# Squared sums for the weights' scales, a two-step split of v, and a list-scheduled first block in an attention and mixture-of-experts kernel

## The chip, the cores and the metric

The kernel runs on one core of a Trainium2 chip. The core has five engines with an instruction queue each: TensorE (PE in the profile, with its weight loads apart as PEld), VectorE (DVE), ScalarE (ACT), GpSimd (POOL) and SyncE (SP), which issues the DMAs here. An engine takes its instructions strictly in the order in which they were written into its queue, and waits where an operand isn't there yet. The metric is the device time of one execution in microseconds (us); the time of a kernel is the median of its runs.

## What is computed

Attention on 4 batches, 8 heads, 768 positions and 64 elements a head: each position sees its neighbours (closer than 16) and a summary of each block of 32 keys. Its output, 3072 rows of 512, goes through four dense experts that are mixed by given weights.

```python
scores_l = scale * q @ k.T                      # only where |i - j| < 16
scores_s = scale * q @ k_sum.T + log(32)        # k_sum: the maximum over each block of 32
a = softmax([scores_l, scores_s])
x = a @ [v, v_sum]                              # v_sum: the mean over each block
p = domain_probs / domain_probs.sum(-1)
for e in range(4):
    out += p[:, e:e + 1] * (relu(x @ w1[e]) @ w2[e])
```

The result has to be close to float32, so the kernel splits operands into a high and a low part of a shorter type, and makes three matrix products in place of one.

## The kernel before

Attention works in pieces: a batch, a block of 96 queries, and a group of four of the eight heads; there are 64, numbered `n` in the order of time, and names such as `ms`, `psc`, `px` carry that number. The experts work on blocks of 384 rows. Blocks 0 and 1 (batch 0) are plain, with operands in 32-bit types: experts 0 and 1 on block 0, then 1 and 0 on block 1. The other work is done for a pair of blocks at once, four experts each, with seven products in place of eight (`SEVEN`) and operands in 16 bits. These need a scale for each matrix, so that the high and low parts fit, and the products are scaled back at the end.

**The first block.** The first eight pieces (`first_tokens`, function `piece`) stand before all expert work and have a form of their own, in plain float32. For a piece TensorE makes scores into two PSUM tiles `psc`, one for the heads in partitions 0 to 63 ("half" 0) and one for those in 64 to 127 (half 1); each score tile gets two matmuls a head, against the keys (128 columns) and against the summary (24 columns). VectorE takes the maximum (`ms`, `nb`), ScalarE the exponential, TensorE turns it (`pT`), multiplies it with v (`pav`), VectorE divides (`xt`), TensorE turns that back, and ScalarE and VectorE split it into `xh` and `xl`. What comes when in this part was written out by hand as keys (`KEYS`, `STEPS`, `T0`), by which the steps are sorted.

**The weights' scales.** `scan` loads a quarter megabyte of a weight matrix into a tile `ws` and takes its largest magnitude into a column of `wmax` (`largest`). After the sixteen tiles of an expert, `scales_of_weights` reduces `wmax` to `wm`, and `scales` makes a maximum over all partitions of it: TensorE transposes `wm` into a PSUM tile `pmw`, VectorE reduces and spreads it, TensorE sends it to all partitions, and eight small VectorE operations make a power of two and its inverse. The experts come in the order 2, 3, 1, 0. With that scale `w1` (tiles `wx`, into `w1g`) and `w2` (tiles `wr`, into `w2g` or `w2s`) are scaled and split.

**v.** For batches 1 to 3 (48 pieces) `stage_a` scales v in place on ScalarE, casts it on ScalarE and makes the low part on GpSimd.

**Order.** Every call is recorded as a `Step` in `program`, and `order_of` makes the queues from that. Each step has a due time that is worked out backwards from TensorE's order, and costs by a table (`takes`, `lasts`); a forward pass picks on each engine the ready step that is due first, a backward pass gives new due times, and of so many rounds the order that ends first by its own reckoning is kept. `in_order` says up to which step an engine keeps the order of the program. In the kernel before that was the whole first block on PE, ACT, DVE and POOL, and the loads of `first_tokens` on SP. Buffers of one tag (`wr` has four, `x` 14, `av` two PSUM banks, `sc` two) are handed out in the order of the program. `ENDS` says how far attention has got at the end of each phase of expert work, `XFREE` up to which piece the odd pieces take tiles from the tag `x`, and `early` how long before a pair's work `x_operands` begins to prepare its operands.

Of the kernel before, what the change touches and what calls it, by code (L numbers as in the profile page):

```python
# [36 lines left out]
SHIFT = 1.12  # L37
ENDS = (17.52,26.5,36.5,53.0,72.0,74.0)
WARM = 11

KEYS = (1.38, 3.85, 1.13, 11.28, 5.91, 6.72, 13.44, 18.09, 21.41, 52.74, 24.82, 23.32, 21.81, 24.25, 59.33, 71.64, 6.83, 9.12)
T0 = 2.57
STEPS = (-1.19, -0.88, 0.85, 0.66, 1.27, 1.34, 1.82, 1.84, 3.16, 3.29, 3.37, 3.66, 3.72, 5.09, 5.84, 6.11, 6.57, 6.89)
CHUNKS = 2
XFREE = 28
NX = 14
# [18 lines left out]
WAIT = dict(PE=53, ACT=33, DVE=33, POOL=76, SP=28)  # L65
SPARE, SPARE_DMA, LANES = 0.1, 300.0, 8
ROUNDS = 10


def columns(ap):  # L70
    return math.prod(n for _, n in ap.ap[1:])
# [15 lines left out]
class Step:  # L87


    def __init__(self, key, issue, op, a, kw):  # L90
        self.key, self.issue = key, issue
        written = [kw[k] for k in ("out", "accum_out") if k in kw]
        read = [x for k, x in kw.items() if k not in ("out", "accum_out")]
        if "out" in kw:
            read += a
        else:
            written.insert(0, a[0])
            read += a[1:]
# [3 lines left out]
        self.behind, self.ahead, self.tiles, self.glued = {}, [], [], False  # L102

    def moved(self):
# [5 lines left out]
    def PE(self, op, kw):  # L110
        n, w = self.moved(), self.read[0]
        if op == "transpose":
            return 95.0, 260.0
        if w.dtype == F32:
            return 65.0 + 1.75 * n, 230.0 + 1.75 * n
        if columns(w) == D:
            return 22.0 + 0.18 * n, 215.0 + 0.25 * n
        t = max(70.0, 0.453 * n) + 15.0 * (n < 200) if w.dtype == F32R else max(45.0, 0.4235 * n)
        t *= 0.65 if w.ap[0][1] == D else 1.0
        return t, t + 165.0  # L120

    def ACT(self, op, kw):
        n = self.moved()
        if op == "activation" and "accum_out" in kw:
            return 420.0 * (1 + SPARE), 560.0 + 420.0 * SPARE
        if op == "mul" and len(self.read) > 1:
# [37 lines left out]
def order_of(steps, bufs, early):  # L164
# [133 lines left out]
    def forward(rank):  # L298
        run = Run(rank, queue, [sum(head[m] != head[n] for m in steps[n].behind) for n in every])
        run.after_slot = lambda n: WAIT[keys[n]]  # L300
        lanes, wire, order = [0.0] * LANES, 0.0, []
        start, end = [0.0] * len(steps), [0.0] * len(steps)
        run.begin()
        while len(order) < len(steps):
            t, k, group = run.next(lambda k: max(run.free[k], lanes[0] + WAIT[k]) if k == "SP" else run.free[k])
            for n in group:
                s = steps[n]
                order.append(n)
                start[n] = t
                if k == "SP":  # L310
# [50 lines left out]
def attn_moe(ctx: ExitStack, tc: tile.TileContext, qvL, qv0, v0L, kD, kT, vT, w1L, w2L, dpL, cst, out):  # L361
# [55 lines left out]

    X_TOP, W1_TOP = 4.0, 0.25
    V_TOP = 256.0
# [5 lines left out]
    def largest(e, fc, which, raw):  # L425
        V.tensor_reduce(
            wmax[:, e, which, fc : fc + 1], raw, axis=AX.X, op=ALU.max, apply_absolute_value=True
        )

# [25 lines left out]
    def scales_of_weights(e):  # L455
        m = sb.tile([P, 2], F32, name=f"wm{e}", tag="wm")
        V.tensor_reduce(m, wmax[:, e], axis=AX.X, op=ALU.max)
        s, back = scales(f"w{e}", m, 2)
        one = const.tile([P, 2], F32, name=f"one{e}")
        V.tensor_scalar_mul(one[:, 0:1], s[:, 0:1], W1_TOP)  # L460
        V.scalar_tensor_tensor(
            one[:, 1:2], back[:, 0:1], 1.0 / (X_TOP * W1_TOP), back[:, 1:2], op0=ALU.mult, op1=ALU.mult
        )
        scale_w[e], back_w[e] = (one[:, 0:1], s[:, 1:2]), one[:, 1:2]

# [142 lines left out]
    def stage_a(n):  # L608
# [205 lines left out]
    def first_tokens(units):  # L814
# [104 lines left out]
        def piece(n, m, s):  # L919
# [11 lines left out]

            def scores(half):
                t["psc", half] = ps_sc.tile([P, 2, 256], F32, name=f"psc{n}_{half}", tag="sc")
                for j in (half, half + 2):
                    o = t["psc", half][:QB, j // 2, :]
                    r = slice((j % 2) * D, (j % 2 + 1) * D)
                    PE.matmul(
                        o[:, 0:KW], qr[r, j // 2, :], kch[2 * g + j // 2][r, w0 : w0 + KW], start=True, stop=True
                    )
                    PE.matmul(o[:, KW:KA], qr[r, j // 2, :], ksr[r, 2 * g + j // 2, :], start=True, stop=True)  # L940

# [62 lines left out]
            def x_part(w):  # L1004
# [6 lines left out]
            steps = (  # L1011
                (v_ones,), (scores, 0), (scores, 1), (maxima, 0), (maxima, 1), (exps, 0), (exps, 1),
                (summary,), (turn, 0), (turn, 1), (turn_summary,), (turned,), (turned_summary,),
# [612 lines left out]
    for (tbs, experts), end in zip(plan, ENDS):  # L1626
# [9 lines left out]
        for e in experts[:1] if paired else experts:  # L1636
# [4 lines left out]
            for us, pace in units:  # L1641
# [84 lines left out]
```

## Time and profile before

| | |
|---|---|
| runs | 1080.18, 1080.83, 1082.72 us; median 1080.83 us |
| profiled execution | 1079.39 us, its span 1077.5 us |
| TensorE clock | 0.995 of full speed in the mean |
| DMA | 194.95 MB, mean 181 GB/s |

The page of the profile gives for each engine its busy time; a view by windows gives the same for chosen stretches, with the granted TensorE clock; the view of waits lists who waited for whom; the view of groups gives the mean duration of one kind of instruction; and the timeline gives instructions with start and duration in us, and in brackets the idle time of the engine ahead of them and what ended it. Almost every instruction has the line L373, the line of a helper, so groups are told apart by the names of tiles.

### The profile page before, as it was taken

To read this page: it belongs to the slowest core of one execution; us is meant where nothing else is said; L and a number is where in the kernel's file an instruction comes from. 1 tells how busy PE (TensorE), PEld (TensorE's weight loads), DVE (VectorE), ACT (ScalarE), POOL (GpSimd) and SP (SyncE) were. 2 spreads that over 40 slices of the span, in tenths; PEclk is the share of its full clock that TensorE was granted. 3 is DMA by queue.
4 is the path that set the end of the run, shared out by engine and by line. 5 is a ranking of instruction groups with operands and counts; after the bars stand their busy time and mean duration, and the time that the engine had idled before them with its cause. 6 is when DMAs were issued, how large, how long until landed. Compare 5 with 4: busy or idle time off the path is not lost.

```text
span 1077.5 us, 22082 instructions
## 1 busy us (share of the span) xinstructions
PE 1051.8 (98%) x7497; PEld 707.7 (66%) x7497; DVE 866.0 (80%) x2102; ACT 730.2 (68%) x1992; POOL 607.2 (56%) x716
## 2 busy tenths in 40 slices
PE   9988999899999999999999999999999999999998
PEld 7977888654554555555555568686775567686867
DVE  6898889988877867988988897998767775969473
ACT  5776688887864744976977796988545763748170
POOL 2599588877743211852856887896532352717050
PEclk9999999989999999999999999999999999999999
DMA  8789887987888889789676664657422440424001
GB/s 287 212 202 244 227 220 198 274 270 198 240 245 253 253 232 254 220 268 263 207 231 170 167 176 126 176 163 217 116 83 89 135 149 16 162 66 151 1 15 59
DMA packets 172897, 194.95 MB, mean 181 GB/s; under 512 B 80368, under 2 KB 117232, under 8 KB 172784
## 3 DMA queue, kind: packets, MB, share of 16 engines
q1 hardware_dynamic: 172784, 193.55, 62.3%
q8 instruction: 58, 0.95, 0.4%
q14 instruction: 55, 0.45, 0.1%
HBM read 141.33 MB, written 35.65 MB: 164 GB/s over the span
## 4 chain that ended last, share of the span: by engine, by line
PE 66%; DVE 5%; POOL 2%; ACT 2%; DMA 1%; issue 1%; SPq 0%; DVEq 0%; POOLq 0%; ACTq 0%
PE po L373 16%; PE phb L373 13%; PE pha L373 8%; PE pob L373 7%; PE poa L373 5%; PE phd L373 4%; PE phc L373 4%; PE poc L373 3%; PE pod L373 2%; PE psc L373 2%; PE px L373 1%; POOL w2g L373 1%; DVE wr L373 1%; DMA wr<-in_w2L 1%; ACT ms L373 0%
## 5 line engine op out<-in xcount | busy, mean ns | idle before, releaser
L373 PEld LDWEIGHTS <-w1g 128*128 128x128 f16 x2352 | 229.2, 98 | 174.2 <-issue 13.0
L373 PEld LDWEIGHTS <-h 128*128 128x128 f16 x1764 | 171.0, 98 | 115.9 <-issue 0.5
L373 PE MATMUL po<-w2s,h 128*128 128x512 f16 x1008 | 239.6, 379 | 0.0
L373 PE MATMUL phb<-x_t,w1g 128*128 128x384 f16 x1008 | 195.3, 327 | 4.6 <-DVE phc L373 1.9
L373 POOL TENSOR_TENSOR w2g<-wr,w2g 128x512 f16<-128x512 f32 (+1 forms) x80 | 90.1, 1133 | 114.3 <-ACT w2g L373 112.1
L373 PE MATMUL pha<-x,w1g 128*128 128x384 f16 x672 | 133.3, 329 | 2.9 <-DVE nb L373 2.9
L373 ACT ACTIVATE ms<-ms,nb 96x152 f32<-96x152 f32 x256 | 104.0, 414 | 15.5 <-DVE nb L373 15.2
L373 PEld LDWEIGHTS <-hs 128*128 128x128 f16 x1008 | 98.0, 98 | 12.7 <-issue 0.4
L373 POOL TENSOR_TENSOR v<-qv,v 128x256 f16<-128x256 f32 (+1 forms) x56 | 45.7, 816 | 104.6 <-ACT v L373 89.7
L373 DVE CUSTOM_DVE_ANT_0 ms<-psc,c_sb 96x152 f32<-96x152 f32 x256 | 69.1, 305 | 31.3 <-PE psc L373 30.5
L373 POOL TENSOR_TENSOR h<-r,h 128x384 f16<-128x384 f32 x56 | 57.1, 1025 | 54.1 <-ACT h L373 51.5
L373 ACT CAST w2g<-wr 128x512 f16<-128x512 f32 (+1 forms) x112 | 61.6, 562 | 32.2 <-DVE wr L373 18.7
L373 POOL TENSOR_TENSOR w<-wr,w 128x512 fp32r<-128x512 f32 x48 | 65.3, 1368 | 26.2 <-ACT w L373 20.3
L373 DVE TENSOR_TENSOR aw<-ms,aw 96x512 f16<-96x512 f32 (+1 forms) x104 | 69.7, 686 | 6.3 <-ACT aw L373 6.3
L373 PE MATMUL ph<-xh,w 128*128 128x384 f32 x256 | 69.4, 343 | 5.1 <-ACT w L373 3.6
L373 PE MATMUL phd<-x_t,w1g 128*128 128x384 f16 x336 | 65.6, 326 | 2.6 <-POOL w1g L373 1.7
L373 PE MATMUL phc<-x,w1g 128*128 128x384 f16 x336 | 66.1, 326 | 0.0
L373 PE MATMUL poa<-w2g,h 128*128 128x256 f16 x504 | 65.4, 273 | 0.4 <-DVE nb L373 0.4
L373 PE MATMUL pob<-w2g,hs 128*128 128x256 f16 x504 | 64.0, 273 | 0.3 <-DVE poc L373 0.3
L373 POOL TENSOR_TENSOR ks<-kr,ks 128x304 fp32r<-128x304 f32 x56 | 53.3, 952 | 16.3 <-ACT ks L373 15.7
L373 PE MATMUL po<-w,hh 128*128 128x512 f32 x192 | 60.8, 396 | 0.0
L373 ACT ACTIVATE wr<-wr,scalew 128x512 f32<-128x512 f32 x72 | 51.8, 719 | 11.2 <-DMA wr<-in_w2L 7.7
(195 smaller groups left out, 2350.1 us busy)
## 6 DMA issues: line engine op xcount, KB each, us to landing
wr<-in_w2L SPq DMA_DIRECT2D x112, 256.0 KB, 3.3
w1g<-wdg SPq DMA_DIRECT2D x34, 512.0 KB, 4.1
w1g<-wdg SPq DMA_DIRECT2D x34, 384.0 KB, 3.8
ws<-in_w1L SPq DMA_DIRECT2D x32, 256.0 KB, 3.8
ws<-in_w2L SPq DMA_DIRECT2D x32, 256.0 KB, 3.8
wx<-in_w1L SPq DMA_DIRECT2D x32, 256.0 KB, 4.7
wdg<-w1g SPq DMA_DIRECT2D x16, 512.0 KB, 4.5
wd<-w2s SPq DMA_DIRECT2D x16, 512.0 KB, 5.1
```

Of the source, the lines that this page charges most:

```text
L373: program.append(Step(self.key, lambda: getattr(self.engine, name)(*a, **kw), name, a, kw))
```

## The change

Seven things are changed.

1. `largest` no longer takes a maximum on VectorE: ScalarE squares the tile and sums it along each row (`accum_out`). `scales_of_weights` then takes the root, as the exponential of half the logarithm, on ScalarE, and adds a floor on VectorE. The tops `W1_TOP` and `W2_TOP` follow from the other measure.
2. For the 48 pieces of batches 1 to 3, v is scaled and cast in one ScalarE operation, and the low part is made in one VectorE operation from the unscaled v. GpSimd has no part in it any more.
3. In the first block `scores` makes both halves in one step, with matmuls that alternate between partitions 0 to 63 and 64 to 127, and that stand glued in TensorE's queue.
4. The first block isn't kept in the program's order on PE, ACT, DVE and POOL: `in_order` is 0 for them. SP's is kept.
5. The rounds of the planner are 24 in place of 10, its reserve on other engines' durations (`SPARE`) is 0.05 in place of 0.1, a switch between tilings of the array costs 80 ns (`SWITCH`), and matmuls of 64 rows cost about half.
6. `ENDS` has attention at 24.5 and 35 pieces, not 26.5 and 36.5, at the end of the second and third phase of expert work (block 1, and the first pair); `XFREE` is 24, not 28.
7. For the first pair, `early` is one more first matrix product.

```diff
-ENDS = (17.52,26.5,36.5,53.0,72.0,74.0)
+ENDS = (17.52,24.5,35,53.0,72.0,74.0)
...
-XFREE = 28
+XFREE = 24
...
-SPARE, SPARE_DMA, LANES = 0.1, 300.0, 8
-ROUNDS = 10
+SPARE, SPARE_DMA, LANES = 0.05, 300.0, 8
+SWITCH = 80
+ROUNDS = 24
...
+                if k == "PE" and s.array != array:
+                    array = s.array
+                    t += SWITCH
...
     def largest(e, fc, which, raw):
-        V.tensor_reduce(
-            wmax[:, e, which, fc : fc + 1], raw, axis=AX.X, op=ALU.max, apply_absolute_value=True
-        )
+        A.activation(raw, raw, AF.Square, scale=ROUND, accum_out=wmax[:, e, which, fc : fc + 1])
...
         V.tensor_reduce(m, wmax[:, e], axis=AX.X, op=ALU.max)
+        V.tensor_scalar_max(m, m, 2.0**-120)
+        A.activation(m, m, AF.Ln)
+        A.activation(m, m, AF.Exp, scale=0.5)
         s, back = scales(f"w{e}", m, 2)
-        one = const.tile([P, 2], F32, name=f"one{e}")
+        one = const.tile([P, 3], F32, name=f"one{e}")
         V.tensor_scalar_mul(one[:, 0:1], s[:, 0:1], W1_TOP)
+        V.tensor_scalar_mul(one[:, 2:3], s[:, 1:2], W2_TOP)
...
-            A.mul(vr, vr, scale_v[b])
-            A.copy(v12[:, :, 0, :], vr)
-            PL.tensor_tensor(v12[:, :, 1, :], vr, v12[:, :, 0, :], op=ALU.subtract)
+            A.mul(v12[:, :, 0, :], vr, scale_v[b])
+            V.scalar_tensor_tensor(v12[:, :, 1, :], vr, scale_v[b], v12[:, :, 0, :], op0=ALU.mult, op1=ALU.subtract)
...
+            def scores():
...
+                for j in range(0, G, 2):
+                    for own in (True, False):
+                        for half in range(2):
+                            r = slice(half * D, (half + 1) * D)
...
+                            PE.matmul(o, qr[r, j // 2, :], keys, start=True, stop=True)
...
-    in_order.update(dict.fromkeys(("PE", "ACT", "DVE", "POOL"), len(program)))
+    in_order.update(dict.fromkeys(("PE", "ACT", "DVE", "POOL"), 0))
...
-                early = first_us if nxt == 3 else first_us + second_us if nxt == 0 else 0.0
+                early = first_us if nxt == 3 else 2 * first_us + second_us if nxt == 0 else 0.0
```

What this does to the queues is seen at three places. The first is TensorE's queue right after the warm-up, the scores of the first piece; `psc_0` is the tile of half 0, `psc_1` that of half 1, `k` keys and `ksr` their summaries. Before:

```order
L373 MATMUL psc_0_117<-k_78,qv_0_82 96x128
L373 MATMUL psc_0_117<-ksr_92,qv_0_82 96x24
L373 MATMUL psc_0_117<-k_79,qv_0_82 96x128
L373 MATMUL psc_0_117<-ksr_92,qv_0_82 96x24
L373 MATMUL psc_1_120<-k_78,qv_0_82 96x128
L373 MATMUL psc_1_120<-ksr_92,qv_0_82 96x24
L373 MATMUL psc_1_120<-k_79,qv_0_82 96x128
L373 MATMUL psc_1_120<-ksr_92,qv_0_82 96x24
L373 MATMUL pvf_121<-vn_101,c_sb 120x256 x2
```

And with the change:

```order
L383 MATMUL psc_0_117<-k_78,qv_0_82 96x128
L383 MATMUL psc_1_118<-k_78,qv_0_82 96x128
L383 MATMUL psc_0_117<-ksr_92,qv_0_82 96x24
L383 MATMUL psc_1_118<-ksr_92,qv_0_82 96x24
L383 MATMUL psc_0_117<-k_79,qv_0_82 96x128
L383 MATMUL psc_1_118<-k_79,qv_0_82 96x128
L383 MATMUL psc_0_117<-ksr_92,qv_0_82 96x24
L383 MATMUL psc_1_118<-ksr_92,qv_0_82 96x24
L383 MATMUL pT_127<-c_sb,ms_119 128x96
```

The halves now alternate matmul by matmul, and one turn of the piece's exponentials stands ahead of the means `pvf`.

The second is SP's queue in the first block, ahead of the first loads for the ninth piece (`kr_113`, and its `qv` behind it). `wr` are weights of expert 0, which wait for one of four buffers, `ws` tiles of the scan, which wait for one of two. Before:

```order
L373 DMA wr_0_108<-in_w2L 128x512
L373 DMA wr_1_109<-in_w2L 128x512
L373 DMA pw<-in_dpL 128x96
L373 DMA ws_1_445<-in_w1L 128x512
L373 DMA ws_1_458<-in_w2L 128x512
L373 DMA wr_2_110<-in_w2L 128x512
L373 DMA ws_2_460<-in_w1L 128x512
L373 DMA ws_2_465<-in_w2L 128x512
L373 DMA ws_3_488<-in_w1L 128x512
L373 DMA wr_3_111<-in_w2L 128x512
L373 DMA kr_113<-in_kT 128x2x128
```

And with the change:

```order
L383 DMA wr_0_108<-in_w2L 128x512
L383 DMA wr_1_109<-in_w2L 128x512
L383 DMA ws_0_412<-in_w1L 128x512
L383 DMA ws_0_425<-in_w2L 128x512
L383 DMA pw<-in_dpL 128x96
L383 DMA wr_2_110<-in_w2L 128x512
L383 DMA wr_3_111<-in_w2L 128x512
L383 DMA kr_113<-in_kT 128x2x128
```

Five scans have moved from the stretch ahead of `kr_113` to behind it, and the two that stood further up have come down into it.

The third is ScalarE's queue where the scale of expert 3 is made, in the first pair's work; `phb`, `p` and `h` are of the products of expert 2, the two `wm_796` are logarithm and exponential. With the change:

```order
L383 COPY phb_2_2_811<-pha_2_2_810 128x384
L383 ACTIVATE ws_7_795,wmax<-ws_7_795 128x512
L383 ACTIVATE h_2_2_794<-phc_2_1_778 128x384
L383 ACTIVATE wr_0_760<-wr_0_760,one_602 128x512
L383 ACT_TABLE_LOAD
L383 ACTIVATE wm_796<-wm_796 128x2
L383 COPY p_2_2_813<-phd_2_2_812 128x384
L383 ACT_TABLE_LOAD
L383 ACTIVATE wm_796<-wm_796 128x2
```

Each of the two small operations has a table load of its own ahead of it, with the copy of a product between them; the same pair of loads stands at the scale of each of the four experts. Before, ScalarE's queue had one table load in all, at the program's start.

More of the change, by code (lines that the diff above doesn't have):

```diff
@@ L42 @@
 T0 = 2.57
-STEPS = (-1.19, -0.88, 0.85, 0.66, 1.27, 1.34, 1.82, 1.84, 3.16, 3.29, 3.37, 3.66, 3.72, 5.09, 5.84, 6.11, 6.57, 6.89)
+STEPS = (-1.19, -0.88, 0.66, 1.27, 1.34, 1.82, 1.84, 3.16, 3.29, 3.37, 3.66, 3.72, 5.09, 5.84, 6.11, 6.57, 6.89)
 CHUNKS = 2
-XFREE = 28
+XFREE = 24
 NX = 14
@@ L102, in __init__ @@
         self.behind, self.ahead, self.tiles, self.glued = {}, [], [], False
+        self.array = (0, 0)
+        if key == "PE" and op == "matmul":
+            w = self.read[0]
+            self.array = w.ap[0][1] == D, columns(w) == D
     def moved(self):
@@ L114, in PE @@
         if w.dtype == F32:
-            return 65.0 + 1.75 * n, 230.0 + 1.75 * n
+            t = (65.0 + 1.75 * n) * (0.53 if w.ap[0][1] == D else 1.0)
+            return t, t + 165.0
         if columns(w) == D:
@@ L124, in ACT @@
         if op == "activation" and "accum_out" in kw:
-            return 420.0 * (1 + SPARE), 560.0 + 420.0 * SPARE
+            t = 420.0 if n < 200 else 175.0 + 0.85 * n
+            return t * (1 + SPARE), t * (1 + SPARE) + 140.0
         if op == "mul" and len(self.read) > 1:
@@ L300, in forward @@
         run.after_slot = lambda n: WAIT[keys[n]]
-        lanes, wire, order = [0.0] * LANES, 0.0, []
+        lanes, wire, order, array = [0.0] * LANES, 0.0, [], (False, False)
         start, end = [0.0] * len(steps), [0.0] * len(steps)
@@ L413, in attn_moe @@
     gsel = [c_sb[:NST, C_G + j : C_G + j + 1] for j in range(3)]
-    X_TOP, W1_TOP = 4.0, 0.25
+    X_TOP, W1_TOP, W2_TOP, ROUND = 4.0, 1.0, 4.0, 1.0 + 2.0**-8
     V_TOP = 256.0
@@ L457, in scales_of_weights @@
         V.tensor_reduce(m, wmax[:, e], axis=AX.X, op=ALU.max)
+        V.tensor_scalar_max(m, m, 2.0**-120)
+        A.activation(m, m, AF.Ln)
+        A.activation(m, m, AF.Exp, scale=0.5)
         s, back = scales(f"w{e}", m, 2)
-        one = const.tile([P, 2], F32, name=f"one{e}")
+        one = const.tile([P, 3], F32, name=f"one{e}")
         V.tensor_scalar_mul(one[:, 0:1], s[:, 0:1], W1_TOP)
+        V.tensor_scalar_mul(one[:, 2:3], s[:, 1:2], W2_TOP)
         V.scalar_tensor_tensor(
-            one[:, 1:2], back[:, 0:1], 1.0 / (X_TOP * W1_TOP), back[:, 1:2], op0=ALU.mult, op1=ALU.mult
+            one[:, 1:2], back[:, 0:1], 1.0 / (X_TOP * W1_TOP * W2_TOP), back[:, 1:2], op0=ALU.mult, op1=ALU.mult
         )
-        scale_w[e], back_w[e] = (one[:, 0:1], s[:, 1:2]), one[:, 1:2]
+        scale_w[e], back_w[e] = (one[:, 0:1], one[:, 2:3]), one[:, 1:2]
     scans = [(e, fc, which) for e in (2, 3, 1, 0) for fc in range(FC) for which in range(2)]
@@ L930, in v_ones @@
                 PL.tensor_copy(t["vf"][:, :, 0:D], qv[:, 2 * QB :].rearrange("p (h d) -> p h d", d=D))
[L932 to L940, printed above, removed]
+            def scores():
+                begin = len(program)
+                room, tag = (ps_mm, "mm") if m in () else (ps_sc, "sc")
+                for half in range(2):
+                    t["psc", half] = room.tile([P, 2, 256], F32, name=f"psc{n}_{half}", tag=tag)
+                for j in range(0, G, 2):
+                    for own in (True, False):
+                        for half in range(2):
+                            r = slice(half * D, (half + 1) * D)
+                            hp = 2 * g + j // 2
+                            o = t["psc", half][:QB, j // 2, 0:KW] if own else t["psc", half][:QB, j // 2, KW:KA]
+                            keys = kch[hp][r, w0 : w0 + KW] if own else ksr[r, hp, :]
+                            PE.matmul(o, qr[r, j // 2, :], keys, start=True, stop=True)
+                for s in program[begin + 1 :]:
+                    s.glued = True
             def maxima(half):
@@ L1011, in piece @@
             steps = (
-                (v_ones,), (scores, 0), (scores, 1), (maxima, 0), (maxima, 1), (exps, 0), (exps, 1),
+                (v_ones,), (scores,), (maxima, 0), (maxima, 1), (exps, 0), (exps, 1),
                 (summary,), (turn, 0), (turn, 1), (turn_summary,), (turned,), (turned_summary,),
```

## The prediction

> **What bounds the kernel now.** I read the page's first part, then the waits of TensorE, then windows of stretches, then timelines where a wait stood out. First the engines over the whole span, and the chain that ended last by engines:
>
> ```profile
> span 1077.5 us, 22082 instructions
> PE 1051.8 (98%) x7497; PEld 707.7 (66%) x7497; DVE 866.0 (80%) x2102; ACT 730.2 (68%) x1992; POOL 607.2 (56%) x716
> PE 66%; DVE 5%; POOL 2%; ACT 2%; DMA 1%; issue 1%; SPq 0%; DVEq 0%; POOLq 0%; ACTq 0%
> ```
>
> TensorE is busy for 1051.8 of 1077.5 us: 25.7 us are all that better feeding alone could win, and the rest only falls if TensorE has less to do. So each edit is weighed by two questions: does it shorten TensorE's own work, and does it remove or add one of its waits? The windows say where it waits; the columns are the stretch, its length, then PE, PEld, DVE, ACT and POOL in us with counts, the granted clock, the share of the DMA engines, and GB/s:
>
> ```profile
> 20.00:40.00 20.00, 19.75 (x173) 17.37 (x171) 17.20 (x74) 14.45 (x42) 3.46 (x7) 1.00 0.52 158
> 40.00:100.00 60.00, 54.65 (x391) 45.70 (x390) 55.87 (x139) 44.98 (x139) 57.47 (x57) 1.00 0.87 227
> 150.00:200.00 50.00, 49.85 (x332) 42.47 (x331) 46.49 (x128) 42.62 (x127) 43.75 (x50) 1.00 0.86 225
> 200.00:225.00 25.00, 18.57 (x115) 11.90 (x114) 24.29 (x53) 20.96 (x64) 19.36 (x24) 0.80 0.92 272
> ```
>
> Up to 40 us TensorE bounds its own stretch. From 40 to 100 it idles 5.3 us while GpSimd is busy for 57.5 of 60, and from 200 to 225 it idles 6.4 us at a clock of 0.80, with VectorE busy for 24.3 of 25. These two hold nearly half of all idle time.
>
> **The first block's scores.** TensorE, pieces two and three; start, duration, form, count:
>
> ```profile
> 12.46 0.46 PE L373 MATMUL psc<-k,qv 64*96 64x128 f32 x2
> 12.76 0.27 PE L373 MATMUL psc<-ksr,qv 64*96 64x24 f32 x2
> 12.87 0.53 PE L373 MATMUL psc<-k,qv 64*96 64x128 f32 x4
> 13.15 0.36 PE L373 MATMUL psc<-ksr,qv 64*96 64x24 f32 x4
> 13.35 0.43 PE L373 MATMUL psc<-k,qv 64*96 64x128 f32 x2
> 13.63 0.27 PE L373 MATMUL psc<-ksr,qv 64*96 64x24 f32 x2
> 13.82 0.68 PE L373 MATMUL pav<-vsf,sT 96*96 96x260 f32 x2
> ```
>
> Two halves happen to meet here. From 12.46 to 12.87 half 1 runs alone (0.41 us for a pair of key and summary products), from 13.35 to 13.82 half 0 alone (0.47), but from 12.87 to 13.35 one pair of each runs, in 0.48. Both halves of the array do work at once. A piece apart takes 2 x (0.41 + 0.47) = 1.76 us, alternating 2 x 0.48 = 0.96: 0.80 less. Eight pieces make 6.4; two pairs already meet (here and in the first piece), which takes off 0.8. So TensorE loses **5.6 us of work** at most. What is late next: a piece's chain through VectorE and ScalarE, and both score tiles now have to be free before the next piece's scores. VectorE is at 17.20 of 20 us in this stretch, of which seven scans at 0.673 (the row is below) are 4.7 and go. So it has room, but TensorE has no other work in the first pieces, and the order shows one turn waiting for exponentials ahead of the means. I take **-4**, bounds -1 and -5.6.
>
> **The stretch from 40 to 100.** TensorE's waits there, two scores of consecutive pieces, and what holds GpSimd up before it:
>
> ```profile
> PE ph L373 <- ACT w L373: 3.6, 3, 1.6
> PE ph L373 <- POOL w L373: 1.4, 2, 0.7
> 16.70 0.46 PE L373 MATMUL psc<-k,qv 64*96 64x128 f32 x2
> 20.47 0.46 PE L373 MATMUL psc<-k,qv 64*96 64x128 f32 x2
> 35.59 0.33 SPq L373 DMA_DIRECT2D wr<-in_w2L  x1
> 35.97 0.43 SPq L373 DMA_DIRECT2D kr<-in_kT  x1
> 41.36 1.04 POOL L373 TENSOR_TENSOR ks<-kr,ks 128x304 fp32r<-128x304 f32 x1 [5.63 <-ACT ks L373]
> ```
>
> TensorE waits 5.0 us for split weights, and GpSimd, which splits them, is full only because it starts late: it is busy for 3.46 us between 20 and 40, then sits 5.63 us until 41.36 for the keys of the ninth piece. Those were issued at 35.97, right behind a `wr` load that had waited for a buffer. In the new order five scans stand behind these loads, not ahead, and ScalarE casts the fourth early tile of w1 two pieces sooner, which frees the buffer sooner. A piece takes 3.8 us (16.70 to 20.47), so I estimate that GpSimd starts some 8 us earlier. Then the work of 57.5 us has 68. I take **-4** of the 5.0, bounds 0 and -5.
>
> **The start of the first pair.** Three waits of TensorE, with the matmul that ended each, and the windows behind them:
>
> ```profile
> 209.63 0.82 PE L373 MATMUL phd<-x_t,w1g 128*128 128x384 f16 x4 [1.70 <-POOL w1g L373]
> 213.21 0.45 PE L373 MATMUL px<-awT,v 128*64 128x192 f16 x4 [2.76 <-DMA awT<-aw]
> 217.21 3.68 PE L373 MATMUL pha<-x,w1g 128*128 128x384 f16 x11 [1.98 <-DVE nb L373]
> 233.69 0.98 PE L373 MATMUL pha<-x,w1g 128*128 128x384 f16 x5
> 214.00:217.00 3.00, 1.23 (x14) 1.13 (x13) 3.00 (x8) 3.00 (x10) 2.92 (x5) 0.50 0.92 255
> 217.00:220.00 3.00, 2.79 (x9) 1.32 (x9) 3.00 (x9) 1.55 (x7) 3.00 (x5) 0.50 0.92 257
> 220.00:223.00 3.00, 3.00 (x13) 1.55 (x12) 2.62 (x5) 1.58 (x7) 0.33 (x1) 0.64 1.10 257
> ```
>
> The waits are 6.4 us. After them the clock is at 0.50: eleven `pha` take 3.68 us, where by the row at 233.69 (five in 0.98, at full clock) 2.2 would do. That is 1.5 us in 3.68; the stretch at a low clock is about twice as long, so some 3 us go. Together **9.4 us**. They come of a pile-up: scales of x, the splits of x, those of w1, and attention, all at once. Four edits thin it out. Attention stands at 24.5 pieces here, not 26.5. x's operands begin one product earlier. VectorE loses the scan and GpSimd the splits of v. And the distance from scores to values is larger in TensorE's order for these pieces, so the DMA behind the 2.76 us has more time. I take **-6**, bounds 0 and -9.4.
>
> **Scans and v on the other engines.** Groups with count, busy us and mean ns:
>
> ```profile
> L373 DVE TENSOR_REDUCE wmax<-ws 128x1 f32<-128x512 f32 x64 | 42.6, 673 | 0.6 <-DMA ws<-in_w2L 0.6
> L373 POOL TENSOR_TENSOR v<-qv,v 128x256 f16<-128x256 f32 x48 | 39.2, 817 | 104.6 <-ACT v L373 89.7 <-DMA awT<-aw 13.6 <-DMA ws<-in_w1L 1.3
> L373 ACT CAST v<-qv 128x256 f16<-128x256 f32 x48 | 19.3, 401 | 13.9 <-PE px L373 13.6
> L373 ACT ACTIVATE wr<-wr,scalew 128x512 f32<-128x512 f32 x72 | 51.8, 719 | 11.2 <-DMA wr<-in_w2L 7.7 <-DVE scalew L373 2.5 <-POOL w2g L373 1.0
> L373 DVE TENSOR_TENSOR w1g<-wx,w1g 128x256 f16<-128x256 f32 x64 | 38.1, 607 | 1.1 <-ACT w1g L373 1.1
> L373 ACT ACT_TABLE_LOAD   x1 | 1.3, 1283 | 0.7 <-PEq L1716 0.7
> ```
>
> VectorE loses 42.6 us and gains 48 low parts, near 0.607 each, 29: it ends 14 lower. GpSimd loses 39. ScalarE gains 64 squares near 0.72, 46, and eight table loads of 1.283, 10, and loses 19 of casts: 37 more, 767 us or 71%. All of it lies beside TensorE in the mean; ScalarE's cover is thinnest from 150 to 225, where it is at 85% now.
>
> **A new wait, on the chain of each expert's scale.** Between `wm` and its transpose on TensorE now stand a floor, two small ScalarE operations and two table loads: 2.6 us of loads alone. How much room is there? VectorE's `wm` and the transpose `pmw`, of experts 1 and 0:
>
> ```profile
> 415.67 0.16 DVE L373 TENSOR_REDUCE wm<-wmax 128x2 f32<-128x16 f32 x1
> 416.52 0.27 PE L373 MATMUL pmw<-c_sb,wm 128*2 128x128 f32 x1
> 493.04 0.16 DVE L373 TENSOR_REDUCE wm<-wmax 128x2 f32<-128x16 f32 x1
> 493.65 0.27 PE L373 MATMUL pmw<-c_sb,wm 128*2 128x128 f32 x1
> ```
>
> 0.7 and 0.5 us. The planner puts the transpose where its table expects `wm`, and the table knows no table load. So TensorE stands at `pmw` for up to 2.6 us at each of four places, with all its matmuls queued behind it, and ScalarE's exponentials, casts and PSUM copies stand behind the loads. The first load of a pair has nothing to wait for and can run while ScalarE idles, and an engine running ahead of the plan eats some more. I take half of 2.6 and a little, 1.5 at each: **+6**, bounds 0 and +10.4.
>
> [...]
>
> **Less reserve, other order.** TensorE's waits behind 230 us are of nine kinds and 7.0 us together; the first and the last of them (sum, count, longest):
>
> ```profile
> PE phb L373 <- DVE phc L373: 1.9, 3, 0.9
> PE phb L373 <- DVE w1g L373: 0.2, 1, 0.2
> ```
>
>  Another order may lose or remake them; a smaller reserve lets the plan run nearer to what an engine can do, so that more of it comes late. I take 0, bounds -3 and +6.
>
> **The sum.** 1079.4 (the profiled execution) - 4 - 4 - 6 + 6 + 0 = 1071.4. The median of the runs lies 1.4 us over that execution, so I predict **1073**.
>
> **Rivals.**
> - *All of the waits go and the table loads hide*: -5.6 - 5 - 9.4 with nothing for the scales, 1079.4 - 20 + 1.4, **1061**. For it: leads in the order grow at all three places. Against: `pmw` has under a microsecond of room.
> - *Table loads end on top*: slower. One mechanism, at four places: TensorE stands at `pmw`, ScalarE's backlog keeps the next products waiting, and the clock drops as it did at 214, which cost 3 us. A place then costs 2.6 + 3 = 5.6, four 22, in place of my 6: 1073 + 16, **1089**. It decides from 14/4 = 3.5 us a place, where the gains are eaten. For it: ScalarE is at 85% there. Against: a wait of 1.6 us between 40 and 100 left the clock at 1.00 in the mean, and at 214 two waits of 1.70 and 2.76 lay within 6 us. [...]
> - *The change doesn't do what it says*: the row tiles save TensorE work that it then spends waiting for VectorE, GpSimd's earlier start is used up by the next loads, and the pile-up moves with the pair. Then -1, 0, -3, +4: **1081**.
>
> **Chances.** Forecast 44%, the better rival 22%, no difference 14%, the slower one 20%. A measurement of this kernel can tell about 0.2%, 2.2 us, from no change. The first two lie below 1078.7: faster 66%, same 14%, slower 20%. The bounds of the terms alone go from 1058 (every lower end: 1080.8 - 5.6 - 5 - 9.4 - 3) to 1096 (every upper end: 1080.8 - 1 + 10.4 + 6). For 8 in 10 I leave out the tails of both: **1060 to 1088**.
>
> **What would show it.** In the new profile the first eight pieces' scores should take near 0.96 us each with four or eight matmuls merged in the timeline, and `pav` of the eighth piece end 3 to 5 us sooner. GpSimd's `ks` of the ninth piece should start near 33 us, not 41. Waits in 40 to 100 should be 1 to 2 us, those at the first `phd` under 3 and the clock there 1.00. Four waits of PE `pmw` for ACT `wm` should stand in the view of waits, 1 to 2.6 us each, with ACT_TABLE_LOAD x9. I am wrong if the waits around 50 to 100 stay, if waits over 3 us at `pmw` come with a clock of 0.50, or if new waits for ScalarE appear between 100 and 260.

## The result, and the profile after

| | before | with the change |
|---|---|---|
| median | 1080.48 us (10 runs) | 1092.98 us (10 runs, 1084.37 to 1095.76) |
| ratio | | 1.010, 95% interval 1.008 to 1.012 |
| profiled execution | 1079.39 us, span 1077.5 us | 1092.43 us, span 1090.6 us |
| mean TensorE clock, runs | 0.995 (profiled) | 0.985 to 0.987 in seven runs, 0.995 to 0.998 in three |

The kernel is slower by 12.5 us, where 7.8 us faster was forecast. The runs of the new kernel fall in two groups by their mean clock: seven at 1092.4 to 1095.8 us (mean 1093.9), three at 1084.4 to 1086.4 us (mean 1085.3). The groups differ by 8.6 us, and the profile is of the first kind. One run each of experiments 4 (1788.9 us) and 16 (2158.3 us) took far longer than the other nine; it counts in the median below and is left out of groups, means and clocks.

The first lines of the page and three groups of it (count, busy us and mean ns):

```profile
span 1090.6 us, 22122 instructions
PE 1056.5 (97%) x7497; PEld 709.1 (65%) x7497; DVE 855.3 (78%) x2094; ACT 758.1 (70%) x2088; POOL 582.2 (53%) x668
L383 ACT ACTIVATE ws<-ws 128x512 f32<-128x512 f32 x64 | 40.1, 627 | 0.0
L383 ACT ACT_TABLE_LOAD x9 | 11.5, 1283 | 0.9 <-PEq L1733 0.7
L383 DVE SCALAR_TENSOR_TENSOR v<-qv,vscale,v 128x256 f16<-128x256 f32 x48 | 30.8, 641 | 0.7 <-ACT v L383 0.6
```

The work of the engines moved as forecast, by some two thirds to three quarters of the sizes (-14, -39 and +37): VectorE is 10.7 us lower, GpSimd 25.0, ScalarE 27.9 higher. GpSimd did lose the 39.2 us of v whole, but its other groups took 14 us more in sum; a square on ScalarE took 627 ns where 720 were reckoned with. TensorE is *busy* 4.7 us longer, though it has less to do. The windows of the changed kernel say why (stretch, length, busy time of PE, PEld, DVE, ACT, POOL, clock, DMA share, GB/s):

```profile
20.00:40.00 20.00, 19.01 (x119) 16.20 (x119) 11.72 (x46) 12.09 (x36) 6.71 (x10) 0.53 0.50 144
40.00:100.00 60.00, 58.12 (x412) 50.88 (x412) 52.28 (x141) 48.09 (x147) 54.18 (x57) 0.99 0.86 225
200.00:225.00 25.00, 24.45 (x168) 16.26 (x167) 23.04 (x56) 24.14 (x74) 21.12 (x26) 1.00 0.84 246
225.00:300.00 75.00, 66.99 (x445) 36.39 (x443) 67.31 (x162) 64.84 (x182) 52.76 (x64) 0.98 0.80 219
600.00:800.00 200.00, 192.91 (x1609) 137.33 (x1607) 167.09 (x398) 142.63 (x394) 132.99 (x134) 0.99 0.56 149
```

And the two of these stretches of the kernel before that were not shown yet:

```profile
225.00:300.00 75.00, 72.58 (x488) 40.12 (x487) 65.42 (x169) 62.90 (x176) 56.59 (x75) 1.00 0.81 232
600.00:800.00 200.00, 198.56 (x1662) 143.46 (x1661) 165.50 (x398) 151.07 (x419) 142.50 (x152) 1.00 0.55 153
```

The reader is to see two gains and three losses. TensorE's idle time from 40 to 100 us fell from 5.3 to 1.9 us, and from 200 to 225 from 6.4 to 0.6, there with a full clock in place of 0.80. But **from 20 to 40 us the clock is at 0.53**, and TensorE does in these 20 us 119 matmul records where it did 173. And it idles 5.6 us more than before from 225 to 300, and 5.6 us more from 600 to 800.

The first block in TensorE's timeline of the changed kernel, with its waits, and the same kinds of matmul ahead of 21 us and behind:

```profile
8.74 0.30 PE L383 MATMUL pT<-c_sb,ms 96*128 96x96 f32 x1 [1.84 <-ACT ms L383]
...
13.68 0.65 PE L383 MATMUL pav<-vsf,sT 96*96 96x260 f32 x2 [0.66 <-ACT ms L383]
...
15.40 0.46 PE L383 MATMUL psc<-k,qv 64*96 64x128 f32 x4
...
16.33 0.68 PE L383 MATMUL pav<-vsf,sT 96*96 96x260 f32 x2
...
20.98 1.13 PE L383 MATMUL pav<-vsf,sT 96*96 96x260 f32 x2 [0.86 <-DVE sT L383]
...
32.02 0.74 PE L383 MATMUL psc<-k,qv 64*96 64x128 f32 x4
```

All scores of a piece stand between 15.40 and 16.33: 0.93 us, as forecast (0.96). No wait is over 1.84 us. At 20.98 a wait of 0.86 ends, and from then on the same work takes 1.6 times as long or more (0.74 us for 0.46, 1.13 for 0.68). The half clock lasts from 21.07 to 41.55 us, 20.5 us; without it the mean clock of this execution would be 0.996 in place of 0.987, which is that of the three faster runs.

### The profile page after: what moved, and what is told of

It is laid out like the page before. It is cut to its first block, busy times and chain, and to the rows that moved or that the text cites. A ratio compares the mean times of both kernels' runs of the same rounds, so it can differ in the third digit from the quotient of the medians.

```text
span 1090.6 us, 22122 instructions
## 1 busy us (share of the span) xinstructions
PE 1056.5 (97%) x7497; PEld 709.1 (65%) x7497; DVE 855.3 (78%) x2094; ACT 758.1 (70%) x2088; POOL 582.2 (53%) x668
## 4 chain that ended last, share of the span: by engine, by line
PE 69%; DVE 14%; ACT 7%; POOL 4%; issue 3%; DMA 1%; SPq 0%; DVEq 0%; POOLq 0%; ACTq 0%
PE po L383 20%; PE phb L383 10%; PE pob L383 7%; PE pha L383 6%; PE ph L383 4%; PE poa L383 4%; PE phc L383 3%; PE phd L383 3%; PE psc L383 3%; PE poc L383 2%; PE pod L383 2%; ACT ms L383 2%; DVE s L383 2%; PE px L383 2%; DVE wr L383 2%
## 5 line engine op out<-in xcount | busy, mean ns | idle before, releaser
L383 POOL TENSOR_TENSOR w2g<-wr,w2g 128x256 f16<-128x256 f32 (+1 forms) x80 | 90.7, 1141 | 129.2 <-ACT w2g L383 126.9
L383 PE MATMUL pha<-x,w1g 128*128 128x384 f16 x672 | 130.6, 327 | 0.7 <-DVE nb L383 0.4
L383 POOL TENSOR_TENSOR qs<-qv,qs 128x192 fp32r<-128x192 f32 x56 | 37.7, 673 | 105.0 <-ACT qs L383 99.5
L383 POOL TENSOR_TENSOR w<-wr,w 128x512 fp32r<-128x512 f32 x48 | 68.2, 1428 | 17.1 <-ACT w L383 16.9
L383 POOL TENSOR_TENSOR hs<-s,hs 128x384 f16<-128x384 f32 x44 | 46.8, 1073 | 22.1 <-ACT hs L383 21.9
```

The costliest lines, as they stand in the source:

```text
L383: program.append(Step(self.key, lambda: getattr(self.engine, name)(*a, **kw), name, a, kw))
```

## The experiments

The time is the median beside that of the kernel before on the same chip (1080.3 to 1082.3 us). Four theories stood at first: A, the half clock of the first block comes of TensorE's waits there and is most of the loss; B, it comes of matmuls in both halves of the array at once; C, the table loads are the loss; and for what is left, late waits of other causes.

**1. Fill the first block's waits.** The order stays; matmuls that nobody reads go behind two steps:

```diff
+FILL0, FILLG = 16, {2: 7}
...
+                psc_of[m] = t["psc", 0]
+                if m == 0:
+                    fill[len(program) - 1] = [psc_of[0]] * FILL0
...
+                if m in FILLG:
+                    ahead_of[len(program)] = [psc_of[m + 1]] * FILLG[m]
                 PE.matmul(t["pv"], t["sT"], vsf[g], start=True, stop=False)
...
+    def busy(tiles):
+        for p in tiles:
+            tc.keep_in_program_order(
+                nc.tensor.matmul(p[:QB, 0, KA : KA + QB], ident[:, :QB], ident[:, :QB], start=True, stop=True)
+            )
```

> The changed kernel in its own order, with 16 idle-time matmuls (96x96, into unused columns of a score tile) behind the first piece's scores, where TensorE waits 1.84 us, and 7 ahead of the third piece's values, where it waits 0.86 us. Theory A (the waits of the list-scheduled first block drop the clock to 0.50 from 21 to 41.5 us, and that half clock is most of the loss): no 0.50 stretch between 20 and 41 us, mean clock 0.995 or more, 1084 to 1086 us against 1093. Theory B (matmuls in both halves of the array at once drop the clock): the 0.50 stretch stays, 1092 to 1095 us.

Measured: 1089.6 us (1088.1 to 1090.3), all four runs at 0.993 to 0.995. Window of its profile:

```profile
20.00:40.00 20.00, 19.00 (x193) 16.03 (x192) 16.60 (x79) 18.41 (x57) 10.93 (x13) 1.00 0.57 162
```

The half clock is gone in every run though the row tiles are there, against B. The time is 4 us above the forecast of A, and above the three runs of the changed kernel without the drop. Three shorter drops stayed (3.4 us each, at 228, 467 and 716 us, 1.7 us of time each; the changed kernel has two of these), and the first turn (`pT`) comes at 11.58 us, where it came at 8.74: behind the filling, which writes into a score tile, TensorE still waits 0.87 us for the exponentials. How much of the 4 us that is was not taken apart.

**2. The hand-written order back** (`in_order` at `len(program)` for all four engines, row tiles kept).

> The changed kernel, but the first block stays in the program's order on PE, ACT, DVE and POOL, as before the change; row tiles and all else stay. Theory A: TensorE's waits before 21 us fall from some 4.7 us to under 2.5, no 0.50 stretch before 41 us, clock 0.995 or more, 1081 to 1087 us. Theory B: the row tiles are still there, so the 0.50 stretch stays, 1090 to 1095 us.

Measured: 1101.1 us, clock 0.984 to 0.989; in the profile the clock is at half from 23.6 to 50.9 us. A's forecast for this run was wrong: with the order by hand TensorE still idles 3.9 us up to 20 us (1.8 in the kernel before), so the list order is not what makes the waits and drops the clock.

**3. Scores half after half**, list-scheduled (the two loops over `half` and `j` exchanged).

> The changed kernel, but the scores of the first block run half after half, as before the change; it is still list-scheduled. Theory A: the first piece still waits for its exponentials, the clock still drops in most runs, 1090 to 1098 us. Theory B: with no two halves at once the clock stays at 1.00 between 20 and 41 us, and the 5.6 us of row tiles are lost, 1086 to 1092 us with a clock of 0.995 or more.

Measured: 1095.4 us (1092.7 to 1099.6). Neither forecast was met. The profile has one window of 3.4 us at half clock in the first block, at 8.9 us, then 1.00 up to 49.9, and five more such windows behind that; three runs have a mean clock of 0.991 or 0.992, one of 0.981. So without row tiles the long drop seems rarer (one run of four), but four runs don't settle how much.

**4. No logarithm, no exponential** (both are `AF.Copy`), in the same order.

> The changed kernel in its own order with the logarithm and the exponential of the scales replaced by two copies of the same size, which leaves out the root; eight table loads of 1.283 us go. Theory C (the table loads, with the waits of 2.6 us at pmw and what stands behind them, are the loss): 1080 to 1084 us, nearly all of the 12 us. Theory A: the clock still drops before 41 us in most runs, and 2 to 5 us are gained, 1088 to 1091 us; in runs without the drop 1080 to 1083.

Measured: 1086.0 us; six runs with the drop have a mean of 1086.3, three without it 1077.4. Against 1093.9 and 1085.3 with the loads that is **7.6 and 7.9 us** for eight loads (1 us more if it is reckoned from the kernel before, which took 1.0 us more on this chip). Theory C has that part and not the rest: the runs with the drop are 9 us above those without it, here too.

**5 to 8.** Next, the root without a table: two VectorE operations on the bits, at the same places of the same order, alone (5), with the filling of 1 (6), and with the planner's old reserve and rounds as well (7). And the loads alone, put into the kernel before (8).

```diff
-        A.activation(m, m, AF.Ln)
-        A.activation(m, m, AF.Exp, scale=0.5)
+        nc.vector.tensor_scalar(mi, mi, 1, None, op0=ALU.logical_shift_right)
+        nc.vector.tensor_scalar(mi, mi, 0x1FC00000, None, op0=ALU.add)
```

```diff
-SPARE, SPARE_DMA, LANES = 0.05, 300.0, 8
+SPARE, SPARE_DMA, LANES = 0.1, 300.0, 8
...
-ROUNDS = 24
+ROUNDS = 10
```

> The changed kernel in its own order, with the root made by two small VectorE operations on the bits (a shift by one, an addition) at the places of logarithm and exponential; no table load is left but the first. If the eight loads cost what the run without the root showed, 1085 to 1088 us in runs in which the clock drops before 41 us, and 1076 to 1080 where it doesn't. Rival (the root as such, or its place on VectorE, costs): 1088 to 1093.

> The same, and the idle-time matmuls of the first experiment in the first block (16 behind the first piece's scores, 7 ahead of the third piece's values). If table loads and the half clock of the first block are two losses that add up, no 0.50 stretch between 20 and 41 us and 1076 to 1080 us in all runs, below the kernel before (1081). Rival (TensorE's other new waits are the real loss, and whatever is won early is waited for later): 1084 to 1088.

> As the second of these, with the planner's reserve back at 0.1 and its rounds at 10. If the smaller reserve makes the late waits of 225 to 300 us and 600 to 800 us (phb for VectorE's phc, some 12 us together against 4 before), they fall to 6 or less and the time to 1070 to 1076. Rival (these waits come of the other order as such): 1076 to 1084, with other waits in their place.

> The kernel before in its own order, with a logarithm and an exponential of wm behind its reduction at each expert's scale, which leaves the value as it was: the eight table loads alone. If the loads cost 7 us of the change, 1086 to 1090 us, with TensorE waiting 2 to 3 us at each pmw but the first. Rival (they cost only where ScalarE is full, as it is with the squares): 1081 to 1084.

Measured: 5, 1083.5 us: six runs at 0.984 to 0.989 with a mean of 1086.2, four at 0.996 to 0.998 with 1077.4, as forecast. 6, 1082.3 us (1079.0 to 1084.6), no long drop, but above its range: here the filling waited for the constants (1.1 us for their DMA), which in that run came late. 7, 1079.9 us, above its range, with a drop of 10.2 us at 34.6 us, behind a wait of 1.46 us; that is the range of its rival. 8, 1090.9 us against 1082.2, ratio 1.009 (1.006 to 1.012): the loads alone cost **8.7 us**. Waits of TensorE in 8:

```profile
PE pmw L374 <- ACT wm L1671: 7.3, 3, 3.4
```

2.4 us in the mean at three places, 3.4 at the worst, and none for `wm` at the first: about the 2.6 us that the working of the forecast had as the most, and once more than that.

**9 to 12.** The first of these is run 7 with the filling at that order's waits; the next two undo one part each in it, and the last puts the row tiles alone into the kernel before.

```diff
-ENDS = (17.52,24.5,35,53.0,72.0,74.0)
+ENDS = (17.52,26.5,36.5,53.0,72.0,74.0)
...
-            A.mul(v12[:, :, 0, :], vr, scale_v[b])
-            V.scalar_tensor_tensor(v12[:, :, 1, :], vr, scale_v[b], v12[:, :, 0, :], op0=ALU.mult, op1=ALU.subtract)
+            A.mul(vr, vr, scale_v[b])
+            A.copy(v12[:, :, 0, :], vr)
+            PL.tensor_tensor(v12[:, :, 1, :], vr, v12[:, :, 0, :], op=ALU.subtract)
```

> The third of the last four (no table loads, reserve 0.1, 10 rounds) in the same order, with the idle-time matmuls put where its trace has waits in the first block: 8 behind the first piece's scores, from operands that are there (not the constants), 14 ahead of the turns of the fourth and of the eighth piece's output, which wait 1.46 and 1.32 us. If the half-clock stretches of 10.2 and 3.4 us and the misplaced matmuls are what that kernel still loses, 1071 to 1076 us with a clock of 0.996 or more. Rival (time won in the first block is waited for later): 1078 to 1081.

> The same with ENDS, XFREE and the early start of the first pair's operands as before the change. If these thin out the pile-up at the start of the first pair, as forecast, TensorE loses some 5 us or more between 200 and 225 us again, and loses less between 600 and 800 us (5.6 us of lead lost there now); the total 1075 to 1082. Rival (the moved ends do nothing at 200 to 225, v and the scans do): under 2 us lost there, total 1070 to 1075.

> As the first of these four, with v scaled, cast and split in three operations on ScalarE and GpSimd, as before the change. If the low parts of v on VectorE are what makes phc late between 600 and 800 us, the lead lost there falls from 5.6 to under 2.5 us. Rival (another cause): 4 to 7 us as before, and more idle time between 40 and 100 and 200 and 225 us, where GpSimd is full; the total 1076 to 1084.

> The kernel before with the first block's scores in row tiles alone, in the order by hand. If the tiles save TensorE's work and the other engines follow, 1075 to 1079 us. If TensorE then waits for VectorE and ScalarE instead, 1079 to 1083 at a clock of 0.994; if the waits are also enough to drop the clock, as with the changed kernel in that order, a half-clock stretch of 20 us or more before 50 us and 1086 to 1094.

Measured: 1086.5, 1084.9, 1089.0 and 1090.6 us. The first three missed: the clock dropped in the first block of all three profiles (17.1, 23.9 and 23.9 us long). In 9 the filling wrote into the tile of the outputs, and so waited for the same VectorE division as the step behind it: it starts at 30.76 us behind a wait of 1.47, and the clock drops at 31.1. In 10 and 11 the orders are others, and the filling came too late: it starts at 33.8 and 34.8 us, and the clock had dropped at 23.5 and 22.5, behind a wait of 0.85 and 0.86 us for `sT` that nothing filled. One reading holds all the same: with the old `ENDS` TensorE is busy 18.26 us of 200 to 225, without it 23.30.

The row tiles alone cost 8.3 us (ratio 1.0105, 1.006 to 1.015), with the order by hand and no table load:

```profile
0.00:20.00 20.00, 14.59 (x78) 9.34 (x79) 7.50 (x29) 5.84 (x14) 2.69 (x13) 0.79 0.92 326
20.00:40.00 20.00, 19.39 (x111) 15.64 (x110) 11.60 (x47) 8.36 (x25) 4.73 (x14) 0.50 0.25 78
```

The clock is at half from 8.1 to 14.9 us and from 18.3 to 59.3. Up to 20 us TensorE idles 5.4 us, against 1.8 before.

**13 to 15.** The old first block (halves, order by hand) in the changed kernel; with the root on VectorE and the old reserve; and with the old v.

> The changed kernel with the first block as before the change on all engines (scores half after half, order by hand); everything else of the change stays, the table loads too. If the half clock of the first block, which comes of row tiles and list order, is what puts the change behind, no half-clock stretch of over 7 us before 50 us, 1081 to 1086 us against 1093. Rival (the drop is chance, or the block pays in another way): 1088 or more.

> The same, with the root by two small VectorE operations (no table loads) and with reserve and rounds as before the change. If the three losses add up (first block 8, loads 7 to 8, reserve 3 to 5 us), 1070 to 1076 us, below the kernel before by 6 to 11: the scans on ScalarE, v and the moved ends are then a gain. Rival (what is won at 40 to 100 and 200 to 225 us is waited for later): 1078 to 1082.

> The second of these with v scaled, cast and split in three operations on ScalarE and GpSimd. If v's low parts on VectorE cost 5 us between 600 and 800 us and win 2 to 3 at the start of the first pair, 1 to 3 us faster than the second: 1068 to 1075. Rival (they win what they cost, or more): 1073 to 1080.

Measured: 1094.1, 1088.9 and 1083.5 us, all above their ranges. In the first and the third the clock is at half for 10.2 us all the same, from 33.7 and 38.1 us, so the old block alone doesn't keep the clock up there. In the second the clock stays at 1.00 to 95 us, and still nothing is won: TensorE is busy 53.40 us of 40 to 100, less than before. With the old block GpSimd starts the `ks` of the ninth piece at 48.4, 43.9 and 51.9 us; in run 5, with the new block and no drop, at 34.6:

```profile
34.61 0.92 POOL L383 TENSOR_TENSOR ks<-kr,ks 128x304 fp32r<-128x304 f32 x1 [1.68 <-ACT ks L383]
```

So the gain of 40 to 100 us hangs on the new form of the first block, and undoing the block was no clean way to take away its drop. It is more the list order than the row tiles: run 3, list-scheduled and half after half, starts that `ks` at 39.5 us, and run 2, with row tiles and the order by hand, at 51.6.

**16 to 18.** Fill the waits with matmuls that wait for nothing: the warm-up's own, with its zeros and its tile. In the order of the changed kernel (16), with the old reserve and rounds (17), and with the old `ENDS`, `XFREE` and early start too (18). All have the root on VectorE.

```diff
+FILL0, FILLG, FILLX = 8, {0: 2, 2: 3}, {}
...
+                if m == 0:
+                    after_of[len(program) - 1] = FILL0
...
+            tc.keep_in_program_order(nc.tensor.matmul(pz, z[:, 0:P], z, start=True, stop=True))
```

> The changed kernel in its own order, the root on VectorE (no table loads), and the first block's waits filled with warm-up matmuls (zeros, 128x512, into the warm-up's own tile, so that they wait for nothing): 8 behind the first piece's scores, 2 and 3 ahead of the values of the first and the third piece. If the half clock of the first block comes of these waits, no half-clock stretch before 41 us in any run and 1076 to 1080 us, against 1077 and 1087 in the two kinds of runs without the filling. Rival (filling does not decide it): 1082 to 1088 in half of the runs or more.

> The same with reserve 0.1 and 10 rounds, in the order of the run that had these; 8, 2 and 1, and 6 ahead of the turn of the fourth piece's output, where that order waits 1.46 us. If the late waits of 225 to 300 us come of the small reserve, 1070 to 1076 us. Rival (its loss before 45 us is the order's, not the clock's): 1077 to 1081.

> The second of these with ENDS, XFREE and the early start as before the change; 8, 2 and 3, and 3 ahead of the turn of the second half's means. If the moved ends only move a wait (won at 200 to 225 us, lost again at 600 to 800), within 3 us of the second, with TensorE idle 5 us or more at 200 to 225 and under 2 between 600 and 800. Rival (they are a net gain): 5 us or more slower than the second.

Measured: 16, 1079.2 us (1077.5 to 1081.1 in nine runs), clock 0.995 or more in all nine: the group at 1086 is gone. 17, **1075.7 us against 1081.0, ratio 0.9945 (0.993 to 0.996)**, faster than both kernels (1071.4 us at a clock of 0.999 to 1079.1 at 0.994, so drops are not gone). 18, 1076.1 us. The stretch from 225 to 300 us in 16 and 17:

```profile
225.00:300.00 75.00, 68.56 (x474) 37.34 (x474) 71.14 (x170) 63.37 (x182) 54.60 (x66) 1.00 0.81 227
```

```profile
225.00:300.00 75.00, 72.54 (x503) 40.35 (x502) 71.10 (x177) 67.92 (x192) 56.30 (x66) 1.00 0.91 250
```

With the old reserve and rounds 4 us of idle time are gone there, about as much as the time falls (3.5). The orders differ, and so does the filling. And 200 to 225 and 600 to 800 us, of 17 and then of 18:

```profile
200.00:225.00 25.00, 23.33 (x171) 14.68 (x170) 23.05 (x62) 23.48 (x72) 18.07 (x26) 1.00 0.96 251
600.00:800.00 200.00, 195.04 (x1644) 141.77 (x1643) 170.85 (x397) 145.31 (x399) 129.62 (x137) 1.00 0.56 151
```

```profile
200.00:225.00 25.00, 18.62 (x106) 11.13 (x106) 21.08 (x44) 19.85 (x62) 17.65 (x22) 0.80 0.83 246
600.00:800.00 200.00, 198.70 (x1671) 144.14 (x1669) 168.83 (x401) 146.00 (x403) 134.04 (x138) 1.00 0.56 153
```

The moved ends win 4.7 us of idle time and a clock of 1.00 in the first stretch and lose 3.7 us in the second; the totals differ by 0.4 us. In these two orders they move a wait and win nothing in the end.

## Why the prediction was wrong

**The step that failed: "What is late next", of the row tiles.** The prediction saw that both score tiles must be free and that the first pieces have no other work, and took 1.6 us off a gain of 5.6 for it. It priced these waits at their own length. They cost the clock. The half clock behind them is 8.6 us in seven of ten runs (1093.9 against 1085.3), and it goes when the waits are filled (16). The term was forecast as -4, with bounds of -1 and -5.6; it came out as a loss of some 6 us.

**What the clock goes by.** Within the span the trace of the kernel before has changes of the clock at 211.91 and 222.15 us, and that of the changed kernel at 21.07, 41.55, 232.69, 236.11, 717.39, 720.80 and 1089.44. From one change to the next it is 3.41 us or a whole multiple of it (10.24 is three, 20.48 six), so the spans are cut here into windows of 3.41 us that meet these changes. The window ahead of a drop in the kernel before, and five windows of the changed kernel:

```profile
208.50:211.91 3.41, 0.82 (x4) 0.31 (x4) 3.41 (x8) 3.02 (x8) 3.41 (x4) 1.00 0.75 185
...
17.65:21.07 3.42, 2.42 (x27) 1.75 (x26) 2.27 (x14) 3.25 (x11) 2.66 (x5) 1.00 0.64 188
21.07:24.48 3.41, 3.41 (x19) 2.86 (x21) 2.23 (x6) 1.40 (x5) 0.65 (x2) 0.50 0.86 277
24.48:27.89 3.41, 3.28 (x29) 2.60 (x26) 2.37 (x13) 2.22 (x8) 0.16 (x1) 0.50 0.10 32
...
38.13:41.55 3.42, 3.42 (x18) 3.25 (x15) 1.37 (x9) 1.59 (x4) 0.00 (x0) 0.50 0.53 159
41.55:44.96 3.41, 3.41 (x29) 3.00 (x29) 2.53 (x10) 3.27 (x11) 2.20 (x3) 1.00 0.35 93
```

In the changed kernel TensorE is busy 71% of the window ahead of the drop (2.42 of 3.42 us), and 96 to 100% of the six windows at half clock, so the busy share of a window doesn't decide. In the kernel before it was busy for 0.82 of 3.41 us ahead of the drop: the clock fell at 211.91 us, in the middle of the wait of 2.76 us, and not behind the three waits, as the prediction read it. The prediction looked for a drop with the change at `pmw` alone.

A count that fits these two traces: add up, over the matmul records that start in a window, the columns, times the rows used of 128, twice for plain fp32 (`ph`, `po` and the later scores `psc<-ks,qs` are fp32r and count once). Behind 7 us the two traces have 630 whole windows within their spans, and the fullest counts 8,448. In the 12 that had a clock of 0.50 in the window behind them the count is 3,048 or less, in the other 618 it is 3,072 or more. That is fitted to these two traces, not a law: if each record is shared out over its duration, one window is on the wrong side. The counts, by the windows' starts:

```text
first block, before (10.5 to 34.4 us, full clock)      3,244 to 4,348
with the change, window ahead of the drop (17.65)      2,518
with the change, at half clock (21.1 to 34.7)          2,096 to 2,688
with the change, at half clock (38.1, with six ph)     3,414, and the clock returns
```

The first block is light work: scores use 64 rows of 128, most of the rest 96. At full clock the kernel before counts 3,244 or more in each window; in the changed kernel the window of 17.65 has 1.0 us of idle time, 0.86 of it one wait, and counts 2,518 (2,518 in 2.42 us of work would be some 3,560 in a full window, an estimate). At half clock the same matmuls take 1.6 times as long or more (0.74 us for 0.46), and windows that TensorE fills to 96 to 100% count 2,096 to 2,688: the block did not get back by its own work, and stayed slow until expert products came. With the row tiles alone (run 12) a piece takes 6.20 us at half clock (25.26 to 31.46); it counts 4,044, some 2,220 in a window, an estimate. The windows begin 0.59 us behind the start of the trace of the changed kernel, and 0.28 in that of the kernel before; that this makes the two groups of runs was not shown. Row tiles go with a full clock too (run 1 has them at 1.00 from 20 to 40 us); but they took away work of TensorE while VectorE and ScalarE set the pace, and alone (run 12) they left it idle for 5.4 us up to 20 us, against 1.8.

**The terms, one by one.**

- *Row tiles, -4*: TensorE's work fell as worked out (0.93 us a piece). With no drop at all (run 5) it idles 5.1 us up to 40 us, 3.1 more than before, so of 5.6 us about 2.5 are left; with the drop, which costs 8.6, it is a loss of 6. The last `pav` of the first block, which was to end 3 to 5 us sooner than at 40.2 us, ends at 42.2 without the drop and at 50.2 with it.
- *40 to 100, -4*: right. 3.5 us of idle time are gone. `ks` was to start near 33 us; it does at 34.6 without the drop, at 42.4 with it. The cause was half told: SP's order alone doesn't do it (43.9 or later with the old first block).
- *First pair, -6*: 5.9 us of idle time and the half clock of 10.2 us went, more than forecast. But the moved ends, which were to thin out the pile-up, give back 3.7 us between 600 and 800 (17 against 18), and the totals are the same. No term had looked so far ahead.
- *Table loads, +6, 0 to +10.4*: 7.6 and 7.9 in the changed kernel, 8.7 in the kernel before. Size and place were right, the form only partly. TensorE waits at `pmw` for `wm` at one place, of the four that were forecast; at another for the spread of it (`dgw`), at a third for ScalarE's copy of a product, and at one for nothing. Against run 4, the same order without the loads, it idles 1.2, 1.4, 2.1 and 0 us more at these four (225 to 245, 140 to 170, 460 to 480, 380 to 400), 4.7 us together; where the rest of the 7.6 goes isn't shown.

```profile
PE pmw L383 <- ACT wm L383: 2.6, 1, 2.6
PE phb L383 <- ACT phb L383: 2.1, 1, 2.1
PE pmw L383 <- DVE dgw L383: 1.4, 1, 1.4
PE phb L383 <- DVE phc L383: 5.7, 9, 1.1
```

  The last row, 1.9 before the change, is the largest wait and not a matter of the loads: without them it is 6.9 (4) and 6.7 (16), and with the old `ENDS`, `XFREE` and early start and the old reserve 0.9 (18).

  The two loads of the place with `wm`, and the wait on TensorE that ends with them:

```profile
228.28 1.28 ACT L383 ACT_TABLE_LOAD   x1
229.58 0.20 ACT L383 ACTIVATE wm<-wm 128x2 f32<-128x2 f32 x1
229.69 0.46 ACT L383 COPY p<-phd 128x384 f32<-128x384 f32 x1
230.17 1.28 ACT L383 ACT_TABLE_LOAD   x1
231.46 0.20 ACT L383 ACTIVATE wm<-wm 128x2 f32<-128x2 f32 x1
```

```profile
231.72 0.27 PE L383 MATMUL pmw<-c_sb,wm 128*2 128x128 f32 x1 [2.62 <-ACT wm L383]
```

  Behind each load the next operation starts 0.01 to 0.02 us later, at the other three places as well.
- *Less reserve, 0, -3 to +6*: 3.5 us (16 to 17, reserve and rounds together), a cost, within the bounds.

**The sum.** 8.6 for the half clock, 7.7 for the table loads and 3.5 for reserve and rounds make 19.8 us of losses, if the three add up; they were measured in different orders. The kernel is 12.5 us slower, so the rest of the change would be a gain of 7.3; the kernel without the three (17) is 5.3 us faster than before, its filling included. The slower rival (1089) had the right sign and the right kind of mechanism, and a drop of one window (3.4 us) did come behind the wait at `pmw` of 231.72, but the one that decided was in another stretch.

**What stays open.** Each edit also lets the planner make another order, and runs 13 to 15 show that this alone is worth some us. Why TensorE idles 7.1 us between 600 and 800 us is not settled (waits for VectorE's `phc` are 1.9 of them): with the old ends it is 1.3 (18), and the run with the old v (11) had 1.6, but with other orders. The two parts of less reserve, `SPARE` and `ROUNDS`, were not tried apart.

## What to carry to other kernels

Price a wait of TensorE by what it does to the clock, not by its length: in a stretch of light matmuls (few rows, small tiles) count what is streamed between the points at which the traces of the kernel show the clock to change (3.41 us apart or a multiple here), and where it comes near what they show ahead of a drop (3,048 or less here), make the work that is taken off TensorE there good, by warm-up matmuls in the waits if need be (with them the slower group of runs was gone in run 16). Those must depend on nothing, least of all on what the wait is for. And a function that needs another table costs its load: eight of 1.28 us cost 7.6 to 8.7 us here, and 2.6 us of wait on TensorE at one place; a power of two needs no logarithm.

## What the runs showed of the hardware

A clock at half for 20.5 us with TensorE busy for 96% or more of each window (and for 27 and 41 us in experiments 2 and 12, with TensorE busy for 18.74 and 19.39 of the 20 us from 20 to 40): the busy share of the profile didn't tell whether the clock would return. And the drop came behind short waits: none in the window ahead of it was over 0.86 us. A switch of ScalarE's table took 1.28 us at each of eight places, and the next operation started 0.01 to 0.02 us behind it.
